# Three more places for expert weights, and an output written in eighteen contiguous pieces

## The chip, the cores and the metric

The kernel runs on one core of one Trainium2 chip. The metric is device time in microseconds (us). One run is one launch; the time before is 460.35 us, the median of three runs (460.18 to 460.82). What the host does before and after the launch, such as putting rows in order, is not part of the time.

## The reference, cut to what matters

Three layers follow one another, all in float32. `B`, `H`, `S`, `D`, `M` are 8, 8, 576, 64, 32.

```python
# 1: attention over 32 memory rows per head
a = softmax(phi)                                    # (8, 8, 576, 32)
k_m, v_m = einsum('bhsm,bhsd->bhmd', a, k), einsum('bhsm,bhsd->bhmd', a, v)
x = softmax(q @ k_m.T / 8) @ v_m                    # then to 4608 tokens x 512
# 2: maxout layer, 512 -> 768 -> 512
x = maximum(maximum(x @ w1, x @ w2), x @ w3) @ w_out
# 3: eight experts with four slots each
logits = x @ phi2                                   # 4608 x 32
slot_input = softmax(logits, axis=0).T @ x          # 32 x 512, four rows for each expert
slot_out[e] = maximum(slot_input[e] @ e_w1[e], 0) @ e_w2[e]     # 512 -> 1024 -> 512
out = softmax(logits, axis=1) @ slot_out            # 4608 x 512
```

The expert weights are 32 MB, the output is 9.4 MB. Each expert's weights meet only four rows, so the experts are little arithmetic on many bytes.

## The kernel before, in words

**The main part** (up to about 384 us of the trace) runs layers 1 and 2. Its order is written out by hand in the string `ORDER`, which names small steps one after another; each step issues a few instructions, and an engine works through its own in that order. Matmuls of `mn` (L597) fill it.

**Expert weights** are cut into 64 pieces of 512 KB, each 128 partitions by 4 KB in DRAM. The list `order` says in which sequence they are used: four `in` pieces of an expert (`e_w1`), then two `a` pieces of the expert before (the left 256 columns of `e_w2`), and at the very end sixteen `b` pieces, two for each expert (the right 256 columns). A piece goes to place `k % NSLOT` of the list `slots`. The helper `send(n)` (L279 to L287) issues the next n pieces on SP, the engine whose queue carries all transfers of this kernel; the step `send 1` in `ORDER` calls it. Places become available one after another: two of `extra` and seventeen of `arena` first, then the `late` ones, then `more2` once the pools of the main part are closed, a stretch of `hbuf` after the last sums over slots, and `wo` after the last use of the output weights of layer 2. There are 41 places, so pieces 41 to 63 reload the first 23 places when TensorE has read them. One place is a list of four buffers of 1 KB to a partition, each filled by a transfer of its own (L284). SP waits for nothing but what an instruction needs (its buffer to be free, and the transfer eight before it to have landed), and in its queue one waiting transfer holds up all behind it.

**After the main part** the last softmax over tokens is closed (L843 to L948), and the expert loop runs: `ex_in(e)` (L1016) multiplies the slots with `e_w1`, `ex_turn` transposes the result, `ex_out(e, 0)` (L1033) multiplies with the `a` pieces; one step of the softmax over slots (`c_first`, `c_second`, `c_last1`, `c_last2`) stands in each turn.

**The end** is the loop at L1110 to L1121. `so_a(x)` and `so_b(x)` (L1053, L1058 to L1060) bring half x of `slot_out` (256 columns) into two tiles `sh` and `sl`. `ex_out(r, 1)` multiplies with the `b` pieces of expert r. `st_out(r, x)` makes the rows of part r (512 tokens) and half x of the output: 12 matmuls (L1082, L1086) into four PSUM banks `x` of the pool `ps_x`, four evictions of 128x256 (two on ScalarE, L1095, two on VectorE, L1093), and a store on SP. For r below 6 each half is stored by itself (L1106: 512 KB in rows of 1 KB); for r = 6, 7, 8 both halves are collected first and stored in rows of 2 KB (L1099, L1104). The first loop runs `ex_out(r, 1)` and `st_out(r, 0)` in turn, the second `st_out(r, 1)` for all nine r. Since `ps_x` has four banks, a `st_out` takes the banks of the one before it.

Of the kernel before, what the change touches and what calls it, by code (L numbers as in the profile page):

```python
# [7 lines left out]
FP32 = mybir.dt.float32  # L8
# [14 lines left out]
for _x in (2, 3, 4, 5, 12, 6, 7, 13, 8, 9, 14, 15, 10, 11):  # L23
# [3 lines left out]
NX = 6  # L27
# [131 lines left out]
)  # L159
W = [1, 0, 0, 3, 2]  # L160
LL = 0
VP = 3
EXTRA = 2
NSLOT = EXTRA + 9 + 12 + NX + 2 + 3 + 3 + 1 + 3


@with_exitstack
def kernel(
# [87 lines left out]
    slots = [extra[:, PIECE * j:PIECE * j + PIECE] for j in range(EXTRA)]  # L256
    slots += [arena[:, o:o + PIECE] for o in slot_off]
    late_slots = [h5x[:, 0:PIECE]] + [arena[:, PIECE * j:PIECE * j + PIECE] for j in range(9)]
    late_slots += [hbuf[:, 2, 0:PIECE], arena[:, x0:x0 + PIECE]]

    order = [("in", 0)]
    for e in range(E):
# [15 lines left out]
    def send(n):  # L278
        for _ in range(n):  # L279
            if sent[0] < len(pieces):  # L280
                x = slot(sent[0])
                if isinstance(x, list):
                    for g in range(4):
                        nc.sync.dma_start(out=x[g], in_=pieces[sent[0]][:, 256 * g:256 * g + 256])  # L284
                else:
                    nc.sync.dma_start(out=x, in_=pieces[sent[0]])
                sent[0] += 1  # L287
# [519 lines left out]
    with tc.manual_schedule():  # L807
# [34 lines left out]

        main_x.close()  # L843
        more2 = ctx.enter_context(tc.tile_pool(name="more2", bufs=1, side="right"))
        more2_sb = more2.tile([128, 3 * PIECE], FP32, name="more2")
        slots.extend(more2_sb[:, PIECE * j:PIECE * j + PIECE] for j in range(3))
        send(3)
        L = B - 1
        st_logit(L, 5)
        last_logit(LL, 6)  # L850
# [62 lines left out]
        for x in range(2):  # L913
            y = mx()
            for i in range(3):
                nc.tensor.matmul(
                    y[:, 32 * i:32 * i + 32], s_run[:, 128 * (3 * x + i):128 * (3 * x + i) + 128], wsel,
                    start=True, stop=True)
            if x:
                nc.vector.tensor_copy(out=st[x], in_=y[:, 0:96])  # L920
            else:
                nc.scalar.activation(out=st[x], in_=y[:, 0:96], func=ACTF.Copy)
        nc.vector.memset(msk, 0.0)
        warm(W[2], True)
        seen = set()
# [127 lines left out]
            nc.vector.tensor_copy(out=so_sb, in_=acc[x][:, 0:256])  # L1053

        def so_b(x):
            t = mx()
            c = slice(256 * x, 256 * x + 256)
            nc.tensor.matmul(t[:, 0:256], sel, so_sb, start=True, stop=True)  # L1058
            nc.scalar.activation(out=sh[:, c], in_=t[:, 0:256], func=ACTF.Copy)
            nc.vector.tensor_tensor(out=sl[:, c], in0=t[:, 0:256], in1=sh[:, c].bitcast(FP32), op=ALU.subtract)  # L1060

        ov = out.rearrange("(g x s) c -> x s g c", x=2, s=S)
        free = [slots[64 - NSLOT + j] for j in range(NSLOT - (64 - NSLOT))]
        free = [x for x in free if not isinstance(x, list)]

        NH = 6
        tok = {}
        for r in range(9):
            tok[r] = [free.pop(0) for _ in range(1 if r < NH else 2)]

        def st_out(r, x):
            cs = slice(256 * x, 256 * x + 256)
            whole = r >= NH
            if not whole and x == 1 and free:
                tok[r] = [free.pop(0)]
            ts = [mx() for _ in range(4)]
            for k, (c, o) in enumerate(((ch, sh), (cl, sh), (ch, sl))):
                for g in range(4):
                    if r == 8 and g == 3:
                        continue  # L1080
                    rs = slice(32 * g, 32 * g + 32)
                    nc.tensor.matmul(  # L1082
                        ts[g][:, 0:256], c[rs, r], o[rs, cs], start=(k == 0), stop=(k == 2), tile_position=(32 * g, 0))
            if r == 8:
                for k, (c, o) in enumerate(((ch, sh), (cl, sh), (ch, sl))):
                    nc.tensor.matmul(ts[3][:, 0:256], c[:, 9], o[:, cs], start=(k == 0), stop=(k == 2))  # L1086
            for g in range(4):
                if whole:
                    o = tok[r][g // 2].rearrange("p (g c) -> p g c", g=2)[:, g % 2, cs]
                else:  # L1090
                    o = tok[r][0].rearrange("p (g c) -> p g c", g=4)[:, g]
                if g % 2:
                    nc.vector.tensor_copy(out=o, in_=ts[g][:, 0:256])  # L1093
                else:
                    nc.scalar.activation(out=o, in_=ts[g][:, 0:256], func=ACTF.Copy)  # L1095
                if whole and x == 1 and g % 2:
                    o = tok[r][g // 2].rearrange("p (g c) -> p g c", g=2)
                    if r < 8:
                        nc.sync.dma_start(  # L1099
                            out=out[S * r + 128 * g - 128:S * r + 128 * g + 128].rearrange("(g p) c -> p g c", p=128),  # L1100
                            in_=o)
                    else:
                        for y in range(2):
                            nc.sync.dma_start(out=ov[y, 512:576, g - 1:g + 1], in_=o[64 * y:64 * y + 64])  # L1104
            if not whole:
                nc.sync.dma_start(  # L1106
                    out=out[S * r:S * r + 512, cs].rearrange("(g p) c -> p g c", p=128),
                    in_=tok[r][0].rearrange("p (g c) -> p g c", g=4))

        so_a(0)  # L1110
        so_b(0)
        for r in range(9):
            if r < E:
                ex_out(r, 1)
            if r == E - 1:
                so_a(1)
            if r == E:
                so_b(1)
            st_out(r, 0)
        for r in [0, 1, 2, 3, 4, 5, 8, 6, 7]:  # L1120
            st_out(r, 1)  # L1121


# [57 lines left out]
```

## Time and profile before

| What | Value |
|---|---|
| median of three runs | 460.35 us |
| profiled execution, its own time | 462.82 us |
| its span, first to last instruction | 461.0 us |
| TensorE busy | 439.0 us (95%) |
| VectorE busy | 333.3 us (72%) |
| ScalarE busy | 192.4 us (42%) |
| GpSimd busy | 71.4 us (15%) |
| transfers of SP's queue, share of the 16 DMA engines | 65.2% |
| DRAM read and written | 91.38 MB, 17.30 MB |
| mean granted TensorE clock | 0.976 of 2.4 GHz |

The span is what the profiler saw between the first and the last instruction; the profiled execution took 1.8 us more than it, and 2.5 us more than the median of the unprofiled runs. The shares are means over stages with different limits, so the table says what is busy, and only the rows of a stage say what that stage waits for.

### The profile page before, as it was taken

The page shows a single profiled execution, that of the slowest core. Times are in us where ns is not written, and L with a number is a line of the kernel's source. Part 1 is how long each engine was busy: PE and PEld are TensorE (multiplying, and loading weights), DVE is VectorE, ACT ScalarE, POOL GpSimd, SP SyncE. Part 2 cuts the span into 40 slices and gives each one's busy share as a digit, 9 for nine tenths or more (in the row PEclk, how much of TensorE's full clock was granted, in tenths as well). Part 3 has the DMA queues.
Part 4 walks back from the last instruction along what each step waited for, and adds up shares of the span by engine and source line. Part 5 has one row for each costly group of instructions (what it writes and reads, how often), then busy time and mean ns, then how long its engine had stood idle before and what let it go on. Part 6 is the DMA issues. An engine that isn't in the chain of part 4 may idle for free.

```text
span 461.0 us, 12577 instructions
## 1 busy us (share of the span) xinstructions
PE 439.0 (95%) x5233; PEld 363.8 (79%) x5233; DVE 333.3 (72%) x753; ACT 192.4 (42%) x450; POOL 71.4 (15%) x92
## 2 busy tenths in 40 slices
PE   6989999999999999999999999999999999999982
PEld 5778889888887889978889698879878896654461
DVE  1596989879777986798769869899836444595441
ACT  2576766645524343334334334433433313233331
POOL 0235545620020011002100210030200000011000
PEclk9999999999999999999999999999999999999955
DMA  8987894217202395537468675388357775899988
GB/s 318 417 327 276 318 392 150 116 42 309 118 10 112 100 345 180 189 99 256 139 213 291 223 284 181 125 293 292 106 193 251 284 251 213 324 410 407 378 292 276
DMA packets 47657, 109.49 MB, mean 237 GB/s; under 512 B 3440, under 2 KB 26224, under 8 KB 45552
## 3 DMA queue, kind: packets, MB, share of 16 engines
q1 hardware_dynamic: 47600, 108.69, 65.2%
q8 instruction: 41, 0.67, 0.6%
q14 instruction: 16, 0.13, 0.1%
HBM read 91.38 MB, written 17.30 MB: 236 GB/s over the span
## 4 chain that ended last, share of the span: by engine, by line
PE 85%; DVE 5%; DMA 3%; issue 2%; ACT 2%; SPq 1%; POOL 1%; DVEq 0%; ACTq 0%; POOLq 0%
PE m L597 48%; PE x L564 7%; PE l L801 4%; PE x L439 3%; PE x L1082 3%; PE x L748 2%; DMA arena<-in_kv_dram 2%; PE x L475 2%; PE l L680 2%; PE m L1033 2%; PE m L1016 2%; PE x L639 2%; PE x L343 1%; PE l L1033 1%; SPq L663 1%
## 5 line engine op out<-in xcount | busy, mean ns | idle before, releaser
L597 PE MATMUL m<-ah,vh 128*128 128x288 f32 x576 | 171.4, 312 | 1.2 <-DVE ht L611 0.6
L597 PE MATMUL m<-ah,vl 128*128 128x288 f32 x576 | 161.8, 295 | 0.0
L597 PEld LDWEIGHTS m<-ah,vh 128*128 128x128 f32 x576 | 108.2, 188 | 20.6 <-issue 12.4
L597 PE MATMUL m<-al,vh 128*128 128x288 f32 x576 | 123.2, 295 | 0.1
L597 PEld LDWEIGHTS m<-ah,vl 128*128 128x128 f32 x576 | 108.4, 188 | 0.4
L597 PEld LDWEIGHTS m<-al,vh 128*128 128x128 f32 x576 | 92.3, 188 | 0.3 <-POOL al L532 0.3
L607 ACT ACTIVATE g<-m 128x288 f32<-128x288 f32 x96 | 38.9, 410 | 70.8 <-PE m L597 62.5
L609 DVE TENSOR_TENSOR g<-m,g 128x288 f32<-128x288 f32 x96 | 42.5, 449 | 31.0 <-PE m L597 24.4
L573 ACT ACTIVATE vh<-x 128x384 fp32r<-128x384 f32 (+1 forms) x100 | 42.0, 478 | 54.6 <-PE x L564 40.6
L611 DVE TENSOR_TENSOR ht<-m,g 128x288 f32<-128x288 f32 x96 | 42.4, 450 | 20.3 <-PE m L597 9.0
L579 DVE TENSOR_TENSOR vl<-x,vh 128x384 fp32r<-128x384 f32 (+1 forms) x100 | 48.7, 530 | 3.3 <-ACT vh L573 2.8
L564 PE MATMUL x<-arena,kvt 64*32 64x384 f32 (+1 forms) x800 | 39.5, 477 | 1.3 <-DVE vl L579 0.8
L532 POOL TENSOR_TENSOR al<-arena,ah 128x576 fp32r<-128x576 f32 x16 | 23.3, 1465 | 72.1 <-ACT ah L528 42.5
L325 POOL TENSOR_TENSOR arena<-arena 128x768 uint32<-128x768 uint32 (+1 forms) x13 | 23.5, 1808 | 34.5 <-ACT arena L313 24.2
L801 PE MATMUL l<-cst 128*128 128x128 f32 x162 | 25.0, 303 | 3.8 <-DMA cst<-in_consts_dram 3.2
L801 PEld LDWEIGHTS l<-cst 128*128 128x128 f32 x162 | 21.6, 208 | 7.1 <-DMA cst<-in_consts_dram 3.2
L616 POOL COPY arena<-ht 128x64 f32<-128x64 f32 x24 | 6.3, 279 | 124.5 <-DVE ht L611 98.9
L564 PEld LDWEIGHTS x<-arena,kvt 64*32 64x32 f32 x800 | 12.4, 105 | 13.5 <-issue 7.8
L439 PE MATMUL x<-arena 128*32 128x129 f32 x640 | 19.8, 274 | 1.1 <-DMA arena<-in_kv_dram 0.7
L643 DVE STREAM_TRANSPOSE arena<-ht 128x512 f32<-128x512 f32 x30 | 20.5, 697 | 0.2
L439 PEld LDWEIGHTS x<-arena 128*32 128x32 f32 x640 | 17.3, 110 | 3.2 <-DMA arena<-in_kv_dram 0.9
L481 DVE STREAM_TRANSPOSE arena<-x 128x288 f32<-128x288 f32 x32 | 13.3, 457 | 3.7 <-PE x L475 3.7
(246 smaller groups left out, 588.0 us busy)
## 6 DMA issues: line engine op xcount, KB each, us to landing
arena<-in_e_w_dram SPq DMA_DIRECT2D x44, 512.0 KB, 7.7
arena<-in_w_dram SPq DMA_DIRECT2D x14, 768.0 KB, 6.3
arena<-in_kv_dram SPq DMA_DIRECT2D x8, 1290.0 KB, 9.8
arena<-in_q_dram SPq DMA_DIRECT2D x16, 576.0 KB, 6.2
arena<-in_kv_dram SPq DMA_DIRECT2D x8, 1032.0 KB, 6.7
tr<-arena SPq DMA_DIRECT2D x30, 256.0 KB, 3.1
hbuf<-tr SPq DMA_DIRECT2D x30, 256.0 KB, 3.6
arena<-in_phi_t_dram SPq DMA_DIRECT2D x8, 576.0 KB, 5.9
```

The costliest lines, as they stand in the source:

```text
L325: (eng or nc.gpsimd).tensor_tensor(out=du, in0=du, in1=lo.bitcast(U32), op=ALU.add)
L439: nc.tensor.matmul(t[32 * g:32 * g + 32, 0:KVC], phin_sb[:, j, b, 32 * g:32 * g + 32], kv_sb[:, j, b, g] if j < 4 else kv4_sb[:, g], start ...
L532: nc.gpsimd.tensor_tensor(out=al[n][:, :, c], in0=aT_sb[:, :, c], in1=ah[n][:, :, c].bitcast(FP32), op=ALU.subtract)
L564: nc.tensor.matmul(t[b][32 * g:32 * g + 32, 128 * r0:128 * r1], kvt[n][r, b, 32 * g:32 * g + 32], w_sb[r, i, r0:r1, g], start=True, stop=T ...
L573: nc.scalar.activation(out=v1[n, i][0][:, b, c], in_=ph["v1", n, i][b][:, c], func=ACTF.Copy)
L579: nc.vector.tensor_tensor(out=vl[:, b, c], in0=ph["v1", n, i][b][:, c], in1=vh[:, b, c].bitcast(FP32), op=ALU.subtract)
L597: nc.tensor.matmul(t[:, 0:HALF], x, y, start=(k == 0), stop=(k == 5))
L607: nc.scalar.activation(out=g1[u, hf], in_=t[:, 0:HALF], func=ACTF.Copy)
L609: nc.vector.tensor_tensor(out=g1[u, hf], in0=t[:, 0:HALF], in1=g1[u, hf], op=ALU.max)
L611: nc.vector.tensor_tensor(out=ht[n, i][:, cs], in0=t[:, 0:HALF], in1=g1.pop((u, hf)), op=ALU.max)
L643: nc.vector.transpose(out=v, in_=ht[n, i][:, 0:512])
L801: nc.tensor.matmul(t[:, 0:128], ident, ident, start=True, stop=True)
```

## The change

1. There are 44 places. `more2` has five pieces in place of three. The place in `hbuf[:, 2]`, which was among the late ones, now comes after `more2`, and one new list of four buffers (in `s_run` and `h5x`) comes before `wo`.
2. In `ORDER` one `send 1` is gone and one stands later; `send(6)` follows the closing of the pools in place of `send(3)`.
3. The output tensor is `(2, 9, 128, 1024)`: half x, part r, partition, four groups of 256 columns. Each of the 18 pairs (r, x) is stored by one transfer of 128 rows of 4 KB, and the host puts the rows in order.
4. `ex_out(0, 1)` stands ahead of `so_b(0)`; only `st_out(0..3, 0)` stand among the `ex_out(r, 1)`; every second one of the later `st_out` uses the three banks of `ps_m` and the one of `ps_l` in place of `ps_x`.

```diff
@@ ORDER
-    "send 1; lg 7 0; mn 44 0 2; mn 44 0 0; ev 44 0 0; ev 44 1 1; ev 44 1 2; v1h 7 5; mn 44 0 1; ev 44 0 1; ev 44 "
...
+    "43 1 2; ev 43 1 1; ev 43 1 2; hrc 43; mn 45 0 1; ev 45 0 1; trm 6 5; trc 6 5; send 1; mn 47 1 0; v1h 7 4; "
...
+NH = 4
-NSLOT = EXTRA + 9 + 12 + NX + 2 + 3 + 3 + 1 + 3
+NSLOT = EXTRA + 9 + 12 + NX + 2 + 3 + 5 + 2 + 3
...
-    late_slots += [hbuf[:, 2, 0:PIECE], arena[:, x0:x0 + PIECE]]
+    late_slots += [arena[:, x0:x0 + PIECE]]
...
-        more2_sb = more2.tile([128, 3 * PIECE], FP32, name="more2")
-        slots.extend(more2_sb[:, PIECE * j:PIECE * j + PIECE] for j in range(3))
-        send(3)
+        more2_sb = more2.tile([128, 5 * PIECE], FP32, name="more2")
+        slots.extend(more2_sb[:, PIECE * j:PIECE * j + PIECE] for j in range(5))
+        slots.append(hbuf[:, 2, 0:PIECE])
+        send(6)
...
+        slots.append([s_run[:, 512:768]] + [h5x[:, PIECE + 256 * j:PIECE + 256 * j + 256] for j in range(3)])
+        send(1)
...
         def so_b(x):
-            t = mx()
+            t = bank(ps_l, "l") if x else mx()
...
+        def st_out(r, x, pool=None):
             cs = slice(256 * x, 256 * x + 256)
+            if pool:
+                ts = [bank(ps_m, "m") for _ in range(3)] + [bank(ps_l, "l")]
+            else:
+                ts = [mx() for _ in range(4)]
...
+            tok = free.pop(0)
...
-            if not whole:
-                nc.sync.dma_start(
-                    out=out[S * r:S * r + 512, cs].rearrange("(g p) c -> p g c", p=128),
-                    in_=tok[r][0].rearrange("p (g c) -> p g c", g=4))
+            nc.sync.dma_start(out=out[x, r], in_=tok)
 
         so_a(0)
+        ex_out(0, 1)
         so_b(0)
-        for r in range(9):
-            if r < E:
-                ex_out(r, 1)
-            if r == E - 1:
-                so_a(1)
-            if r == E:
-                so_b(1)
-            st_out(r, 0)
-        for r in [0, 1, 2, 3, 4, 5, 8, 6, 7]:
-            st_out(r, 1)
+        for r in range(1, E):
+            ex_out(r, 1)
+            if r <= NH:
+                st_out(r - 1, 0)
+        so_a(1)
+        st_out(NH, 0)
+        so_b(1)
+        st_out(NH + 1, 0, True)
+        rest = [(r, 1) for r in range(9)] + [(r, 0) for r in range(NH + 2, 9)]
+        for i, (r, x) in enumerate(rest):
+            st_out(r, x, i % 2)
```

How the change moves instructions shows at three places. The first is SP's queue from the last transposed tiles of the main part (`hbuf<-tr`) to the reload of `extra`; before it reads:

```order
L286 DMA arena<-in_e_w_dram 128x1024 x3
L645 DMA tr<-arena 128x512
L663 DMA hbuf<-tr 128x4x128 x5
L286 DMA hbuf<-in_e_w_dram 128x1024
L286 DMA arena<-in_e_w_dram 128x1024
L286 DMA more_5414<-in_e_w_dram 128x1024 x3
L286 DMA hbuf<-in_e_w_dram 128x1024
L286 DMA wo<-in_e_w_dram 128x1024 x3
L286 DMA extra<-in_e_w_dram 128x1024 x2
```

In the changed kernel the same stretch reads (`more_5413` is the tile `more2`):

```order
L287 DMA arena<-in_e_w_dram 128x1024
L646 DMA tr<-arena 128x512
L664 DMA hbuf<-tr 128x4x128
L287 DMA arena<-in_e_w_dram 128x1024
L664 DMA hbuf<-tr 128x4x128 x4
L287 DMA arena<-in_e_w_dram 128x1024 x2
L287 DMA more_5413<-in_e_w_dram 128x1024 x5
L287 DMA hbuf<-in_e_w_dram 128x1024 x2
L285 DMA s_run<-in_e_w_dram 128x256
L285 DMA h5x<-in_e_w_dram 128x256 x3
L287 DMA wo<-in_e_w_dram 128x1024 x3
L287 DMA extra<-in_e_w_dram 128x1024 x2
```

The piece for `hbuf`, which stood ahead of one for `arena` and three for `more2`, now stands behind both; two more pieces stand in `more2` and one in the new list, and two of the three `arena` pieces stand behind transfers of transposed tiles.

The second place is the end of SP's queue, the stores of the output; before:

```order
L1106 DMA out_dram<-arena 128x4x256 x6
L1106 DMA out_dram<-more_5414 128x4x256 x2
L1106 DMA out_dram<-hbuf 128x4x256
L1106 DMA out_dram<-wo 128x4x256 x3
L1104 DMA out_dram<-arena 64x2x512 x2
L1104 DMA out_dram<-more_5414 64x2x512 x2
L1099 DMA out_dram<-arena 128x2x512 x3
L1099 DMA out_dram<-hbuf 128x2x512
```

And with the change:

```order
L1093 DMA out_dram<-more 128x1024
L1093 DMA out_dram<-h5x 128x1024
L1093 DMA out_dram<-arena 128x1024 x10
L1093 DMA out_dram<-more_5413 128x1024 x5
L1093 DMA out_dram<-hbuf 128x1024
```

Twenty stores became eighteen of one shape, each of rows of 1024 elements (4 KB), from buffers that are all different.

The third place is TensorE's, around the second `so_b` (the matmul of `hr_96` with `cst`); before:

```order
L1033 MATMUL m<-more,hbuf 32x256
L1082 MATMUL x<-sh,ch 128x256 x4
L1082 MATMUL x<-sh,cl 128x256 x4
L1082 MATMUL x<-sl,ch 128x256 x4
L1058 MATMUL x<-hr_96,cst 128x256
L1082 MATMUL x<-sh,ch 128x256 x3
L1082 MATMUL x<-sh,cl 128x256 x3
L1082 MATMUL x<-sl,ch 128x256 x3
```

With the change:

```order
L1037 MATMUL m<-arena,hbuf 32x256 x20
L1037 MATMUL m<-more,hbuf 32x256 x4
L1081 MATMUL x<-sh,ch 128x256 x4
L1081 MATMUL x<-sh,cl 128x256 x4
L1081 MATMUL x<-sl,ch 128x256 x4
L1062 MATMUL l<-hr_96,cst 128x256
L1081 MATMUL m<-sh,ch 128x256 x3
L1081 MATMUL l<-sh,ch 128x256
L1081 MATMUL m<-sh,cl 128x256 x3
L1081 MATMUL l<-sh,cl 128x256
```

The last three `ex_out` (24 matmuls of 32x256) run without a `st_out` between them, and behind `so_b` the banks of `st_out` alternate between `x` and `m` with `l`.

## Rows read from the trace of the kernel before

**Rows 1.** Windows: start:end, length, busy time (xcount) by engine, granted clock, DMA share, GB/s.
```profile
366.00:382.00 16.00, 16.00 (x125) 15.90 (x123) 6.71 (x15) 4.17 (x10) 0.71 (x3) 1.00 0.67 215
382.00:386.00 4.00, 4.00 (x115) 3.02 (x113) 1.87 (x4) 2.19 (x5) 0.24 (x1) 1.00 0.05 8
386.00:394.00 8.00, 7.15 (x86) 4.50 (x86) 4.07 (x16) 1.77 (x7) 0.00 (x0) 1.00 0.98 385
394.00:396.00 2.00, 2.00 (x24) 1.43 (x13) 1.74 (x2) 0.38 (x1) 0.00 (x0) 1.00 0.46 133
...
400.00:404.00 4.00, 4.00 (x82) 2.43 (x76) 3.60 (x9) 1.40 (x3) 0.00 (x0) 1.00 0.87 322
404.00:426.00 22.00, 20.48 (x362) 11.00 (x354) 16.51 (x47) 7.05 (x19) 3.48 (x4) 1.00 1.03 410
426.00:438.00 12.00, 10.87 (x158) 5.86 (x150) 5.69 (x16) 4.55 (x15) 0.00 (x0) 1.00 1.06 379
438.00:440.00 2.00, 1.46 (x13) 1.15 (x13) 1.07 (x4) 0.97 (x4) 0.00 (x0) 0.68 0.48 167
440.00:452.00 12.00, 10.65 (x84) 8.24 (x84) 4.97 (x14) 4.20 (x14) 0.00 (x0) 0.50 0.95 302
452.00:454.00 2.00, 0.09 (x1) 0.00 (x0) 0.72 (x2) 0.58 (x2) 0.00 (x0) 0.50 0.93 279
454.00:458.00 4.00, 0.00 (x0) 0.00 (x0) 0.00 (x0) 0.00 (x0) 0.00 (x0) 0.50 1.03 384
458.00:461.10 3.10, 0.00 (x0) 0.00 (x0) 0.00 (x0) 0.00 (x0) 0.00 (x0) 0.50 0.41 156
```

**Rows 2.** Chain of waits, 441 to 447 us: start, length, engine, tile, line.
```profile
441.64 1.25 PE x L1082 x10
442.89 0.38 ACT wo L1095
...
443.32 1.25 PE x L1082 x10
```

**Rows 3.** Lines by shape, 440 to 448 us: evictions, xcount, busy, mean ns, idle.
```profile
L1093 DVE COPY wo<-x 128x256 f32<-128x256 f32 x6 | 2.3, 419 | 2.8 <-PE x L1082 2.8
```

**Rows 4.** Timeline of SP's issues, 384 to 462 us: start, length, line, tiles, xcount.
```profile
384.81 0.35 SPq L286 DMA_DIRECT2D hbuf<-in_e_w_dram  x1
...
390.91 0.33 SPq L286 DMA_DIRECT2D hbuf<-in_e_w_dram  x1
394.07 1.28 SPq L286 DMA_DIRECT2D wo<-in_e_w_dram  x3
...
427.71 6.57 SPq L1106 DMA_DIRECT2D out_dram<-arena  x6
```

**Rows 5.** Timeline, VectorE, 383 to 385 us: the main part's last evictions.
```profile
383.58 0.82 DVE L611 TENSOR_TENSOR ht<-m,g 128x288 f32<-128x288 f32 x2 [3.80 <-PE l L680]
```

**Rows 6.** Timeline of TensorE and the halves' tiles, 418 to 422 us.
```profile
418.26 1.07 PE L1033 MATMUL l<-arena,hbuf 128*32 128x256 f32 x16 [0.40 <-DVE hbuf L1025]
...
420.73 0.38 ACT L1059 ACTIVATE sh<-x 128x256 fp32r<-128x256 f32 x1 [0.76 <-PE x L1058]
421.14 0.42 DVE L1060 TENSOR_TENSOR sl<-x,sh 128x256 fp32r<-128x256 f32 x1 [1.21 <-ACT sh L1059]
```

**Rows 7.** Chain of waits, 416 to 438 us.
```profile
419.62 0.32 DVE hr L1053
...
419.99 0.70 PE x L1058 x2
420.69 1.00 PE m L1033 x16
421.69 0.56 PE x L1082 x12
...
431.58 1.93 PE m L1033 x15
```

**Rows 8.** Transfers, 427 to 462 us, in 40 slices: GB/s of each.
```profile
GB/s 397 391 366 379 359 380 384 384 373 377 372 376 293 118 218 349 282 330 276 339 294 335 298 320 334 304 213 248 323 220 307 358 396 407 396 386 302 26 0 0
```

More of the change, by code (lines that the diff above doesn't have):

```diff
@@ L1060, in so_b @@
             nc.vector.tensor_tensor(out=sl[:, c], in0=t[:, 0:256], in1=sh[:, c].bitcast(FP32), op=ALU.subtract)
-        ov = out.rearrange("(g x s) c -> x s g c", x=2, s=S)
         free = [slots[64 - NSLOT + j] for j in range(NSLOT - (64 - NSLOT))]
         free = [x for x in free if not isinstance(x, list)]
-        NH = 6
-        tok = {}
-        for r in range(9):
-            tok[r] = [free.pop(0) for _ in range(1 if r < NH else 2)]
-        def st_out(r, x):
+        def st_out(r, x, pool=None):
             cs = slice(256 * x, 256 * x + 256)
[L1073 to L1076, printed above, removed]
+            if pool:
+                ts = [bank(ps_m, "m") for _ in range(3)] + [bank(ps_l, "l")]
+            else:
+                ts = [mx() for _ in range(4)]
             for k, (c, o) in enumerate(((ch, sh), (cl, sh), (ch, sl))):
@@ L1086, in st_out @@
                     nc.tensor.matmul(ts[3][:, 0:256], c[:, 9], o[:, cs], start=(k == 0), stop=(k == 2))
+            tok = free.pop(0)
             for g in range(4):
[L1088 to L1091, printed above, removed]
+                o = tok[:, 256 * g:256 * g + 256]
                 if g % 2:
@@ L1095, in st_out @@
                     nc.scalar.activation(out=o, in_=ts[g][:, 0:256], func=ACTF.Copy)
-                if whole and x == 1 and g % 2:
-                    o = tok[r][g // 2].rearrange("p (g c) -> p g c", g=2)
-                    if r < 8:
-                        nc.sync.dma_start(
[L1100 to L1104, printed above, removed]
-            if not whole:
-                nc.sync.dma_start(
-                    out=out[S * r:S * r + 512, cs].rearrange("(g p) c -> p g c", p=128),
-                    in_=tok[r][0].rearrange("p (g c) -> p g c", g=4))
+            nc.sync.dma_start(out=out[x, r], in_=tok)
         so_a(0)
+        ex_out(0, 1)
         so_b(0)
-        for r in range(9):
-            if r < E:
-                ex_out(r, 1)
-            if r == E - 1:
-                so_a(1)
-            if r == E:
-                so_b(1)
-            st_out(r, 0)
-        for r in [0, 1, 2, 3, 4, 5, 8, 6, 7]:
-            st_out(r, 1)
+        for r in range(1, E):
[9 more added lines that the diff above has]
+            st_out(r, x, i % 2)
 def kernel(**inputs):
@@ L1175 @@
         args.append(nc.dram_tensor(f"in_{name}_dram", a.shape, _mybir.dt.from_np(a.dtype), kind="ExternalInput").ap())
-    args.append(nc.dram_tensor("out_0_dram", (B * S, DM), _mybir.dt.float32, kind="ExternalOutput").ap())
+    args.append(nc.dram_tensor("out_0_dram", (2, 9, 128, 1024), _mybir.dt.float32, kind="ExternalOutput").ap())
     with _tile.TileContext(nc) as tc:
@@ L1179 @@
     r = _run(nc, [arrays], core_ids=[0])
-    return r.results[0]["out_0_dram"]
+    o = _np.asarray(r.results[0]["out_0_dram"]).reshape(2, 9, 128, 4, 256)
+    res = _np.empty((B, S, 2, 256), f32)
+    res[:, 0:512] = o[:, 0:8].transpose(1, 3, 2, 0, 4).reshape(B, 512, 2, 256)
+    res[:, 512:] = o[:, 8].reshape(2, 2, 64, 4, 256).transpose(3, 1, 2, 0, 4).reshape(B, 64, 2, 256)
+    return res.reshape(B * S, DM)
```

16 rows, old and new, of the table ORDER are left out of this document.

## The prediction

> **What bounds the kernel now.** I read the windows first, stage by stage. Up to 382 us TensorE is busy in every microsecond and the transfers are not (16.00 of 16.00 us at a DMA share of 0.67), so there TensorE sets the time. From 386 us the picture turns: the share is 0.98 to 1.07 in most windows, up to 404 to 426 us, where TensorE rests for 1.5 of 22 us and the transfers run at 410 GB/s [rows 1]. What is left to move from 386 us on is countable: 32 pieces of weights (41 places, of which 32 are filled by then) and an output worth 18 pieces, 50 x 524,288 bytes. At 410 GB/s a piece takes 1.28 us and all take 63.9 us; the last bytes move at 459.5 us [rows 8], after 73.5 us. So the last part is a stream of transfers with 9.6 us lost in it, and the windows say where nearly all of it went, as length x (1 - rate/410) [rows 1]:
>
> - 394 to 396 us at 133 GB/s: 1.35 us, a hole. SP issues one piece at 390.91 us and the next at 394.07 us [rows 4], since each place comes free only then.
> - 386 to 394 us: 0.5 us. 400 to 404 us at 322 GB/s: 0.86 us; no row tells me why.
> - 426 to 438 us at 379 GB/s: 0.9 us. Here the stores in rows of 1 KB begin (issued from 427.71 us [rows 4]), with the engines as busy as they get (1.06).
> - 438 to 440 us at 167 GB/s: 1.2 us, a hole behind `so_b(1)`.
> - 440 to 452 us at 302 GB/s: 3.2 us. This is not the transfers' limit, although their share reads 0.95. The chain of waits shows `st_out` starting every 1.68 us: 1.25 us of matmuls at the half clock, then 0.38 us of eviction on ScalarE before the next may have the banks [rows 2]. 512 KB each 1.68 us is 312 GB/s, just the rate seen.
> - 452 to 459.5 us, stores in rows of 2 KB: 0.64 us and, at 384 GB/s, 0.25 us; then some 0.3 us in the last ragged stretch.
>
> Behind the last bytes lie 1.5 us to the end of the span.
>
> **The change, part by part.**
>
> *Three more places.* 33 pieces are now in by 382 us in place of 32; there is room for the extra one, at a share of 0.67 before 382 us and 0.05 after [rows 1]. The pieces moved behind `hbuf<-tr` let those transfers go sooner, and TensorE waits for neither, so the main part costs nothing more. The first piece in `more2` waits for the main part's pools, whose last user is VectorE's eviction, done at 383.58 + 0.82 = 384.40 us [rows 5]. From SP's issue at 384.81 us to moving bytes at about 386.0 us it takes 1.2 us [rows 1, 4], so the stream starts at 385.6 us, 0.4 us sooner. Seven pieces (five `more2`, two `hbuf`) cover 9.0 us, to about 395 us; `wo` follows at the latest 1.2 us behind 394.07 us plus its issues, and the new list, free after the same matmuls, stands between. Of the hole I leave 0.2 us. The list is one piece in rows of 1 KB: 1.38 us at 379 GB/s, plus 0.1 us. The wait that is added on SP is that of the list for `s_run`: `wo`, `extra` and all reloads stand behind it, but they were waiting for the same stretch of TensorE.
>
> *The stores.* 18 in rows of 4 KB. No row shows a store of that shape. The bounds: 302 GB/s below (the slowest long window of stores) and 410 GB/s above (loads with rows of 4 KB). Between stand 379 GB/s for rows of 1 KB and 384 GB/s for 2 KB, whose best slices reach 396 and 407 [rows 8]. I take 410, 1.28 us each, because the shape is that of the loads and the rate per row grows with its size: 379/1.06 = 358 GB/s per full share with 1 KB, 384/1.03 = 373 with 2 KB, 410/1.03 = 398 with 4 KB [rows 1].
>
> The Trainium skill (page "DMA: Bandwidth & Descriptors", section "Specifications") puts the least size for full line rate at 512 B, so rows of 1 KB would have nothing to gain from being longer. This case's rows speak against that, 358 to 398, but for loads against stores; by the rule the sum would come out 1.4 us later (second rival).
>
> *TensorE's order.* From `ex_out(7, 0)` at 418.26 us [rows 6], with 1.00 us for an `ex_out`, 0.56 us for a `st_out` and 0.70 us for `so_b` [rows 7]: `ex_out(7, 0)` to 419.26; `ex_out(0, 1)` to 420.26, where it covers the wait for VectorE's copy (ready at 419.94 us [rows 7]); `so_b(0)` to 420.96; seven `ex_out` and four `st_out` to 430.20. The tiles `sh` and `sl` (0.38 and 0.42 us [rows 6]) lie beside the next `ex_out`. The wait for late weights, 0.93 us of the last `ex_out` before (1.93 against 1.00 us [rows 7]), goes, since the last load lands by 427.0 us (below). Stores 0 to 3 are thus ready by about 428 us.
>
> Then `st_out(4, 0)` to 430.76, evicted by 431.6 (two evictions on VectorE, 0.42 us each [rows 3]), bytes from 432.8. `so_b(1)` to 431.46; `sh` and `sl` to 432.3; `st_out(5, 0)` needs the bank that `sl` is read from, so it ends at 432.9, is evicted by 433.7 and moves from 434.9 us.
>
> *The banks.* With two sets of banks the 0.38 us between `st_out` go: a store every 1.25 us at the half clock, or every 0.84 us at the full one (two evictions on VectorE). Both are shorter than 1.28 us: transfers bound the rest. No store waits for a buffer, all 18 being different.
>
> **The sum.** The stream: 31 loads and stores 0 to 3 are 35 x 1.28 = 44.8 us from 385.6 us, plus 0.5, 0.2, 0.1 and 0.9 us (the unexplained dip, kept): 432.1 us; the loads alone are through at 427.0 us. A hole of 0.7 us to store 4, which moves from 432.8 to 434.1 us; a second of 0.8 us to store 5. From 434.9 us 13 stores of 1.28 us: 451.5 us. With the ragged 0.3 us and 1.5 us to the end the span is **453.3 us**, 7.7 us under 461.0 us. Counted the other way, by what goes: 1.28 (one piece), 0.4 (start), 1.15 (first hole), 0.9, 3.2, 0.64 and 0.25 (stores), less 0.1 (list) and 0.3 (holes of 1.5 us in place of 1.2): 7.4 us, near enough. The profiled execution itself took 462.82 us, 2.5 us over the median of the runs; I put the difference on the median: 460.35 - 7.7 = **452.6 us**, with 451.0 to 454.3 us for this case by 410 GB/s give or take 3% and the holes give or take 1 us.
>
> Front and end are tied only at 432 to 435 us: a stream that came sooner would just find larger holes there, so the front cannot give more than 0.7 us beyond this, and could lose as much for nothing.
>
> **The rivals.**
>
> - *The rows' size does nothing* (the rule above): stores at 379 GB/s, 1.38 us each. 13 x 0.1 = 1.4 us more, 454.0 us. For it: no 4 KB store in the trace. Chance 0.10.
> - *The clock falls earlier.* Before, it is granted 1.00 in 426 to 438 us and 0.50 from 440 us on [rows 1], after TensorE had short waits; now the waits around `so_b(1)` come at 430 to 433 us. At the half clock `st_out(4, 0)`, `so_b(1)` and `st_out(5, 0)` take 0.69, 0.70 and 0.69 us more, 2.1 us: 454.7 us; the rest still keeps up at 1.25 us. Against: TensorE has no wait before 430.2 us. Chance 0.08.
> - *The places bring nothing*, as the waits only move: the 2.8 us of start, piece and hole come back, the stream reaches store 4 at 434.9 us: 2.1 us less the hole of 0.8 us, 453.9 us. Chance 0.06.
> - *Stores are at their limit already* at 302 GB/s, 1.74 us each, whatever TensorE does. Then 427.0 + 18 x 1.74 + 1.8 = 460.1 us of span, 459.4 us. For it: the share of 0.95 in that window. Against: 379 and 384 GB/s elsewhere, and the 1.68 us. Chance 0.06.
> - *Slower:* sixteen engines write rows 4 KB apart in DRAM, in place of rows 2 KB apart, and hinder one another there. It decides below (461.0 - 1.8 - 427.0)/18 = 1.79 us a store, 293 GB/s. At 270 GB/s, 1.94 us: 463.7 us of span, 463.0 us. Against it: the loads, whose rows lie the same way, run at 410. Chance 0.04.
>
> **How the numbers follow.** The forecast has the remaining 0.66, which includes small mishaps of about 1 us. The predicted time is 452.6 us. The range 450.2 to 457.0 us takes in the forecast's own, the first three rivals and 2 us beyond them for a mixture; it leaves out the last two and the far tails. A run can tell 0.2% (0.9 us) from no change. Faster: all but the slower case and half of the limit at 302 GB/s, and a little for the unforeseen, 0.91; the same 0.05; slower 0.04.
>
> **What would show it.** Right: loads end near 427 us; no window under 300 GB/s between 388 and 431 us; one or two short holes at 432 to 435 us; from there windows near 410 GB/s to about 451 us, with SP, not TensorE, last in the chain. Wrong: stores in long windows at 380 GB/s or less with the share at 1.0 (rows' size); `st_out` spaced by more than 1.3 us with idle transfers between (TensorE still the bound); a hole at 394 us again.

## The result, and the profile after

| | before | changed |
|---|---|---|
| median | 460.59 us (460.18 to 461.87, 4 runs) | 455.0 us (453.61 to 455.64, 4 runs) |
| ratio, with its 95% interval | 1 | 0.9869 (0.9846 to 0.9892) |
| profiled execution, its own time | 462.82 us | 453.61 us |
| its span | 461.0 us | 451.8 us |
| start of `ex_out(7, 0)` to the end of the span | 42.7 us | 35.6 us |
| DRAM read and written | 91.38 MB, 17.30 MB | 91.38 MB, 17.30 MB |

Faster by 5.6 us, inside the range; 452.6 us was forecast, so the gain was put too high. The profiled executions stand 9.2 us apart, more than the medians, and are no typical pair: 462.82 us lies above all 17 runs of the kernel before that stand beside e1 to e4 (459.96 to 462.31 us), and 453.61 us is the fastest of the changed kernel's four. `ex_out(7, 0)`, which began at 418.26 us [rows 6], begins at 416.16 us now: 2.1 us were won in the main part, whose TensorE work the change leaves alone. There the list of waits of the kernel before has two rows that have no counterpart in that of the changed kernel:

```profile
PEld x L439 <- DMA arena<-in_kv_dram: 0.9, 1, 0.9
PE x L439 <- DMA arena<-in_kv_dram: 0.7, 1, 0.7
```

(engine, tile and line, what was waited for, us in all, times, longest). That is 0.8 us near 260 us; the starts of equal matmuls in the two traces drift apart by 0.4 us near 8 us and by 0.7 us near 67 us as well, which makes most of the rest. It is chance and no gain of the change: the wait for `kv` is back with 0.8 or 0.9 us in the profiles of e6 and e7 (experiments, below), which share the changed kernel's main part, and e3, whose main part is that of the kernel before, starts `ex_out(7, 0)` at 417.01 us. So I measure every kernel from the start of `ex_out(7, 0)`, behind all this: 418.26 to 461.0 us before and 416.16 to 451.8 us now are 42.7 and 35.6 us, 7.1 us apart.

The windows of the changed kernel, with the columns of [rows 1]:

```profile
366.00:382.00 16.00, 16.00 (x137) 15.29 (x139) 6.34 (x16) 4.42 (x11) 0.71 (x3) 1.00 0.68 226
382.00:386.00 4.00, 3.85 (x104) 3.06 (x100) 3.04 (x11) 2.06 (x7) 0.24 (x1) 1.00 0.61 190
386.00:394.00 8.00, 7.30 (x88) 4.50 (x80) 4.13 (x9) 1.18 (x4) 0.00 (x0) 1.00 1.04 403
394.00:396.00 2.00, 2.00 (x29) 1.45 (x32) 0.41 (x2) 0.28 (x1) 0.00 (x0) 1.00 0.96 306
...
404.00:426.00 22.00, 21.41 (x378) 11.80 (x382) 15.46 (x45) 7.40 (x21) 3.50 (x4) 1.00 1.03 408
426.00:432.00 6.00, 5.38 (x89) 3.52 (x81) 3.18 (x9) 2.47 (x8) 0.00 (x0) 1.00 0.90 363
432.00:434.00 2.00, 2.00 (x37) 1.95 (x36) 2.00 (x7) 1.93 (x7) 0.00 (x0) 1.00 0.99 397
...
440.00:449.00 9.00, 0.00 (x0) 0.00 (x0) 0.02 (x1) 0.00 (x0) 0.00 (x0) 0.55 1.01 403
449.00:452.00 3.00, 0.00 (x0) 0.00 (x0) 0.00 (x0) 0.00 (x0) 0.00 (x0) 0.50 0.05 19
```

The hole of 133 GB/s at 394 us is gone (306 GB/s is left), and the stretch that ran at 302 GB/s with TensorE busy for 10.65 of 12 us [rows 1] now runs at 403 GB/s with TensorE idle: TensorE is through at 440 us and only transfers are left. In the last 3 us almost nothing moves.

The chain of waits around the second `so_b` (L1062), with start, length, engine, tile and line:

```profile
424.94 2.73 PE m L1037 x48
427.67 0.55 PE x L1081 x11
428.22 0.71 PE l L1062 x2
...
428.95 0.39 ACT sh L1063
...
429.37 0.44 DVE sl L1064
...
431.85 0.66 PE x L1081 x10
...
433.24 0.66 PE x L1081 x11
```

The last three `ex_out` run 2.73 us without a wait for weights, where one alone took 1.93 us [rows 7]. The `st_out` in banks `x` start 1.39 us apart and one in banks `m` and `l` lies between them, so a store's matmuls and evictions take 0.70 us in place of 1.68 us [rows 2]; the clock is 1.00 there.

The rates of 40 slices, 427 to 452 us, in GB/s:

```profile
GB/s 413 426 419 360 302 419 334 131 380 413 413 380 393 419 400 387 400 419 387 380 413 413 413 406 400 393 420 413 406 419 387 426 387 413 406 66 26 13 0 0
```

Two short holes at 429 and 431.5 us, then some 405 GB/s to 448.9 us. The 26 GB/s of the ragged end is one sixteenth of 410, what one of the sixteen DMA engines moves. The packets in the trace say the same: every transfer ends in sixteen packets of 4 bytes, and of those of the last store fourteen lie between 448.9 and 449.2 us, one at 449.6 and one at 450.5 us. Before, they are spread evenly from 458.7 to 459.8 us.

### The profile page after: what moved, and what is told of

The parts are those of the page before. It is cut to its first block, busy times and chain, and to the rows that moved or that the text cites. A ratio compares the mean times of both kernels' runs of the same rounds, so it can differ in the third digit from the quotient of the medians.

```text
span 451.8 us, 12570 instructions
## 1 busy us (share of the span) xinstructions
PE 430.6 (95%) x5233; PEld 359.7 (80%) x5233; DVE 333.5 (74%) x753; ACT 192.5 (43%) x450; POOL 71.4 (16%) x92
## 3 DMA queue, kind: packets, MB, share of 16 engines
HBM read 91.38 MB, written 17.30 MB: 241 GB/s over the span
## 4 chain that ended last, share of the span: by engine, by line
PE 89%; DVE 4%; issue 2%; ACT 1%; POOL 1%; DMA 1%; ACTq 0%; DVEq 0%; POOLq 0%
PE m L598 52%; PE x L565 8%; PE l L802 4%; PE x L440 4%; PE x L749 2%; PE l L681 2%; PE x L476 2%; PE m L1020 2%; PE m L1037 2%; PE x L640 2%; PE x L1081 1%; PE x L344 1%; PE l L1037 1%; PE m L1081 1%; PE x L335 1%
```

## The experiments

Each ran on the chip beside the kernel before, whose median was 461.15 us (17 runs) beside e1 to e4, 461.11 us (12) beside e5 to e8, 461.31 us (7) beside e9 to e11 and 460.67 us (11) beside e12. "Stretch" is span less start of `ex_out(7, 0)` in the timeline of TensorE.

| kernel | median, us | ratio (95% interval) | stretch, us |
|---|---|---|---|
| before | 461.15 | 1 | 42.7 |
| changed | 455.0 | 0.9869 (0.9846 to 0.9892) | 35.6 |
| e1 changed, again | 454.45 | 0.9859 (0.9843 to 0.9875) | 35.7 |
| e2 places alone | 459.73 | 0.9981 (0.9967 to 0.9995) | 41.2 |
| e3 end alone | 458.09 | 0.9947 (0.9926 to 0.9968) | 38.6 |
| e4 six `st_out` ahead | 453.45 | 0.9846 (0.9826 to 0.9866) | 34.6 |
| e5 rows of 1 KB | 457.91 | 0.9922 (0.9905 to 0.9939) | 39.2 |
| e6 four banks | 459.24 | 0.9948 (0.9925 to 0.9971) | 39.6 |
| e7 experts reversed | 454.94 | 0.9874 (0.9846 to 0.9903) | 35.9 |
| e8 reversed, six ahead | 454.29 | 0.9853 (0.9828 to 0.9878) | 35.5 |
| e9 four banks, filled | 454.55 | 0.9851 (0.9813 to 0.9888) | 36.1 |
| e10 no list | 454.07 | 0.9847 (0.9815 to 0.988) | 35.6 |
| e11 eight `st_out` ahead | 454.28 | 0.985 (0.9815 to 0.9885) | 34.4 |
| e12 no list, six ahead | 453.41 | 0.9835 (0.9805 to 0.9865) | 34.8 |

**e1: the changed kernel once more.** No edit; is the gain 5.6 or 9 us?

> The changed kernel once more, for its spread and a second profile. In the first pair of profiles the span fell by 9.2 us, of which 2.1 us lie before 382 us, in code that is the same, at three waits of the main part (about 8, 67 and 260 us; the last is TensorE waiting for a transfer of keys and values). Theory: these 2.1 us are luck of the two profiles, the change is worth what lies behind 382 us, 7 us, and the median of several runs should come to lie 5.5 to 7.5 us under the kernel before; the second profile shows one or more of the three waits again. Rival: the main part really became shorter, then every profile of the changed kernel lacks all three waits and the gain of the medians comes near 9 us.

Its ratio says 6.5 us of 461.15. `ex_out(7, 0)` starts at 417.14 us, 1.0 us later than in the first profile, and the stretch is 35.7 us again. The stretch repeats and the main part does not: of the three waits the one near 8 us is back, those near 67 and 260 us are not.

**e2: the places, with the end of the kernel before.**

```diff
-            t = bank(ps_l, "l") if x else mx()
+            t = mx()
...
-            nc.sync.dma_start(out=out[x, r], in_=tok)
+            if not whole:
+                nc.sync.dma_start(
+                    out=out[S * r:S * r + 512, cs].rearrange("(g p) c -> p g c", p=128),
+                    in_=tok[r][0].rearrange("p (g c) -> p g c", g=4))
...
-        ex_out(0, 1)
-        for r in range(1, E):
...
+        for r in range(9):
+            if r < E:
+                ex_out(r, 1)
```

> The places and their order alone: 44 places and the changed order of the pieces, with the end (stores, banks, order of TensorE) of the kernel before. Theory (stream and TensorE meet only behind the second so_b): the loads land some 2.8 us sooner and the wait of 0.93 us in the last ex_out goes, but behind it a st_out every 1.68 us bounds the end as before, so the gain is 0.9 to 1.5 us, near 459.3 us. Rival (the stream is the bound throughout): 2.8 us, near 457.7 us.

It gains 1.5 us of stretch, as the first theory said (1.4 us by the medians, 0.9 us by the ratio, whose interval reaches from 0.2 to 1.5 us). Chain of waits of e2, whose eviction is L1099 and whose `st_out` is L1086:

```profile
440.12 1.25 PE x L1086 x11
441.38 0.38 ACT more L1099
...
441.80 1.25 PE x L1086 x11
```

Still 1.68 us from one `st_out` to the next. What the earlier stream gave was given back in a wider hole: 271 GB/s in 432 to 434 us and 56 GB/s in 434 to 436 us by the windows.

**e3: the end, with the 41 places and the order of transfers of the kernel before.**

```diff
-NSLOT = EXTRA + 9 + 12 + NX + 2 + 3 + 5 + 2 + 3
+NSLOT = EXTRA + 9 + 12 + NX + 2 + 3 + 3 + 1 + 3
...
-        send(6)
+        more2_sb = more2.tile([128, 3 * PIECE], FP32, name="more2")
+        slots.extend(more2_sb[:, PIECE * j:PIECE * j + PIECE] for j in range(3))
+        send(3)
```

> The end alone: 18 stores of 4 KB rows, two sets of banks, the changed order of TensorE, with the 41 places and the order of pieces of the kernel before. Theory: the stream reaches the fourth store 2.8 us later than with the places, of which about 1 us falls into the holes there; 1.3 to 2 us slower than the changed kernel, near 456.7 us, with loads landing about 2.8 us later and almost no hole behind them. Rival (the places bring nothing, the waits only move): as fast as the changed kernel, 455.0 us. Other rival (the stream has no slack at all): 2.8 us slower, near 457.8 us.

It is 3.0 us slower than the changed kernel by the stretch (38.6 against 35.6) and 3.6 us by the medians (against e1). My theory of 1.3 to 2 us fell; that there is no slack at all, 2.8 us, was right. TensorE's timeline in e3 shows what the late stream does (the `ex_out` is L1034; in brackets the wait and its releaser):

```profile
428.18 0.64 PE L1034 MATMUL m<-more,hbuf 128*32 128x256 f32 x8 [0.67 <-DMA more<-in_e_w_dram]
429.50 0.64 PE L1034 MATMUL m<-h5x,hbuf 128*32 128x256 f32 x8 [0.69 <-DMA h5x<-in_e_w_dram]
```

The last `ex_out` wait for weights, `so_b(1)` behind them comes later, and its hole with it (303 GB/s in 434 to 436 us). So a late front moves the holes along rather than filling them. Places alone 1.5 us, end alone 4.1 us, both 7.1 us: 1.5 us come only from having both.

**e4 and e11: more stores ready before `so_b(1)`.**

```diff
-NH = 4
+NH = 6
```

(7 in e11).

> The changed kernel with st_out(0..5, 0) among the last ex_out in place of st_out(0..3, 0), so that six stores are ready while the stream still moves loads. Theory: the holes behind the second so_b (1.0 us by the windows of the changed kernel's profile, at 429 to 432 us) close, 0.7 to 1.0 us faster than the changed kernel, near 454.2 us. Rival (TensorE's chain sets the end, so_b(1) comes 1.1 us later): no gain, or up to 0.5 us slower.

> The changed kernel with st_out(0..6, 0) among the last ex_out and st_out(7, 0) ahead of the second so_b, nearly the order of TensorE of the kernel before, with the new stores and banks. Theory (with the stream as bound it only matters that stores are ready when the loads end): no holes behind 428 us, as with six ahead, 453.4 us. Rival (the changed order, with the second so_b as early as it can be, is worth something by itself): 454.5 us or slower, with a hole before the stores of the right half.

The holes nearly vanish and the stretch falls by 1.0 and 1.2 us. Windows of e4:

```profile
428.00:430.00 2.00, 2.00 (x40) 1.10 (x36) 1.21 (x4) 1.11 (x4) 0.00 (x0) 1.00 1.03 414
430.00:432.00 2.00, 1.98 (x25) 0.91 (x17) 1.41 (x4) 1.06 (x4) 0.00 (x0) 1.00 1.01 408
432.00:434.00 2.00, 1.39 (x27) 1.17 (x28) 1.25 (x4) 0.95 (x5) 0.00 (x0) 1.00 1.04 422
434.00:436.00 2.00, 2.00 (x38) 1.92 (x37) 1.98 (x6) 1.67 (x6) 0.00 (x0) 0.85 0.94 377
436.00:438.00 2.00, 2.00 (x36) 2.00 (x36) 1.52 (x5) 1.44 (x5) 0.00 (x0) 0.50 1.03 410
```

In the last row the clock is at its lower level, 0.50, and the transfers are still fed: with two sets of banks TensorE keeps up at 1.2 GHz, as the prediction had it. Two `st_out` take 1.68 us there (436.36 to 438.04 us in the chain of waits of e4), so one takes 0.84 us. In e11 the four windows from 428 to 436 us are at 416, 410, 412 and 418 GB/s. The times do not show these gains for certain: the interval of e4's ratio overlaps with that of e1, and e11's median, 454.28 us, lies within 0.2 us of e1's; in its profile `ex_out(7, 0)` starts only at 418.33 us.

**e5: the 18 stores in rows of 1 KB.**

```diff
-            nc.sync.dma_start(out=out[x, r], in_=tok)
+            v = tok.rearrange("p (g c) -> p g c", g=4)
+            nc.sync.dma_start(out=out[S * r:S * r + 512, cs].rearrange("(g p) c -> p g c", p=128), in_=v)
```

(for r = 8, two transfers of 64 partitions).

> The changed kernel, but each of its 18 stores goes to the output as it lay before, in rows of 1 KB (the last part in two transfers each); places, banks and order of TensorE as changed. Theory (the rate grows with the row): from the second so_b on the windows read 375 to 384 GB/s at a full share, 13 stores cost 0.1 us more each, 1.4 us slower than the changed kernel, near 455.9 us. Rival (the Trainium skill, page DMA: Bandwidth & Descriptors, section Specifications: rows of 512 B and more move at full line rate): the same windows near 405 GB/s and the same time, 454.5 us. Third (stores in rows of 1 KB are at their limit at 302 GB/s): 6 us slower.

Windows of e5:

```profile
438.00:440.00 2.00, 2.00 (x36) 1.67 (x35) 1.77 (x6) 1.41 (x6) 0.00 (x0) 1.00 1.05 349
440.00:442.00 2.00, 1.73 (x21) 1.28 (x17) 1.88 (x6) 1.73 (x6) 0.00 (x0) 1.00 1.03 341
...
444.00:446.00 2.00, 0.00 (x0) 0.00 (x0) 0.00 (x0) 0.00 (x0) 0.00 (x0) 0.50 1.04 341
```

The DMA engines are full (1.03 to 1.05) and move 341 to 349 GB/s, where rows of 4 KB get 403: 3.6 us more of stretch, where I expected 1.4. Some 0.6 us of this are hardly the rows': in 448 to 450 us, while a store runs that this edit splits into two transfers, the rate is 242 GB/s at a share of 0.99. The 379 GB/s from which I took that [rows 1] were a price of such stores: from 433 us on, when the last weights were in use, the kernel before moved nothing but stores in rows of 1 KB, at 374 to 385 GB/s in 433 to 437 us. So rows of 1 KB explain a loss near the one I expected, and what takes e5 from there to 341 to 349 GB/s is open; e5 stores right halves of the output in these windows, the kernel before left halves, and no run tests that. The Trainium skill (page "DMA: Bandwidth & Descriptors", section "Specifications") gives 512 B as the least size for full line rate; 1 KB is above that, and these rows do not agree with it. The edit changes the rows' length and their place in DRAM together. The packets of the traces show what the length alone does: at the median one of 1 KB takes 46 ns as a store of the kernel before (428 to 437 us) and as a load for the list in the changed kernel, 48 ns as a store in e5, one of 2 KB 84 ns (stores of the kernel before), one of 4 KB 159 ns as a load and as a store. Sixteen engines with 1024 bytes each 46 ns would move 356 GB/s, with 4096 bytes each 159 ns 412 GB/s.

**e6 and e9: four banks, empty and filled.**

```diff
-        st_out(NH + 1, 0, True)
+        st_out(NH + 1, 0)
+        fill(2)
...
-            st_out(r, x, i % 2)
+            st_out(r, x)
+            fill(2)
```

The two lines with `fill` are in e9 alone; each issues two 128x128 matmuls into a bank that nobody reads.

> The changed kernel with every st_out in the four banks of ps_x, as before. First theory (the banks give back the 3.2 us that the kernel before lost in 440 to 452 us): st_out every 1.68 us at the half clock, 312 GB/s, up to 3 us slower, near 457.5 us. Second theory: at the full clock a st_out takes 0.56 us and the wait for its banks 0.42 us, 0.98 us in all, under the 1.28 us of a transfer, so TensorE runs ahead from 431 us on; if the clock falls at 437 us it has six stores in hand, and the remaining seven at 1.68 us end at 449 us, before the transfers: 0 to 0.5 us slower, 454.5 to 455 us. The spacing of st_out in the chain of waits and windows without holes after 435 us tell.

> The kernel with every st_out in the four banks of ps_x, with two added matmuls of 128x128 into the bank of ps_l behind each st_out from the second so_b on, which nothing reads; they run while TensorE waits for its banks. Theory (four banks lose only together with the half clock: in the profile with four banks the clock fell at 435.7 us and st_out then came every 1.68 us): the clock stays at 1.00 to the end of the st_out, they come every 1.0 to 1.25 us, the windows behind 436 us read 400 to 410 GB/s, and the time is that of the changed kernel, 454.5 to 455 us. Rival (the wait for the banks is the loss at either clock): near 458 to 459 us. If the clock falls all the same, the run decides nothing.

Without the second set of banks 4.0 us are lost, more than the 3 us of the first theory; the second (0 to 0.5 us) fell. Chain of waits of e6:

```profile
433.17 0.99 PE x L1081 x11
434.16 0.38 ACT arena L1092
...
434.58 0.97 PE x L1081 x11
...
437.65 1.25 PE x L1081 x11
438.91 0.38 ACT arena L1092
...
439.33 1.25 PE x L1081 x11
```

The 1.68 us are back. But the matmuls are at half speed there: the clock is 0.85 in 434 to 436 us and 0.50 from then on. At the full clock, from 433.17 to 434.58 us, four banks cost 1.41 us a `st_out`, where the second theory had 0.98 us. e9 keeps the four banks and gives TensorE something to do during each eviction. Its timeline, with the fill on L1098:

```profile
433.70 0.71 PE L1098 MATMUL l<-cst 128*128 128x128 f32 x4
434.34 0.58 PE L1081 MATMUL x<-sh,ch 32*128 32x256 f32 x4
...
435.09 0.71 PE L1098 MATMUL l<-cst 128*128 128x128 f32 x4
```

The clock stays at 1.00 to the end of TensorE's work, a `st_out` with its fill takes 1.39 us (I expected 1.0 to 1.25 us), windows lie mostly at 358 to 399 GB/s (I expected 400 to 410), and only 0.5 us are lost against two sets. All executions agree: the mean clock is 0.974 to 0.978 in all seven of e6 and 0.999 or 1.0 in all four of e9. So four banks cost 4.0 us by two things together, the wait for the eviction (1.41 us in place of 0.70 us) and the half clock that it brings (1.68 us in place of 1.41 us); either cure takes nearly all of it.

**e7 and e8: is the dip at 394 us one of DRAM addresses?** By the bytes moved, pieces 41 to 43 ran slowly before (322 GB/s in 400 to 404 us [rows 1]), and pieces 40 to 42 run slowly after (306 GB/s in 394 to 396 us), 6 to 8 us sooner.

```diff
-        pieces += [e_w1[e, j] for j in range(4)]
+        pieces += [e_w1[E - 1 - e, j] for j in range(4)]
...
-    e_w1 = inputs["moe2_w1"].reshape(E, 4, 128, F)
+    e_w1 = inputs["moe2_w1"].reshape(E, 4, 128, F)[::-1]
```

e8 has this and `NH = 6`.

> The changed kernel with the first-layer expert weights lying in DRAM in reversed order (expert 7 first), used in the same sequence. In four profiles the transfers dip while pieces 40 to 43 move, the first-layer weights of expert 7, whatever the places they go to (400 to 404 us before, 394 to 398 us with the change). Theory (it is where these pieces lie in DRAM): the dip goes, no piece from 41 to 43 takes over 1.32 us, 0.4 to 0.8 us faster, near 453.9 us. Rival (it is the moment: transfers resuming after the main part, or what the engines do then): the dip stays at the same pieces, the same time.

> The reversed order in DRAM and six stores ahead together. Theory: the two gains add, 1.0 us for the closed holes and 0.4 to 0.8 us for the dip, since with the holes closed nothing but the stream sets the end: near 452.9 us. Rival (the dip is of the moment): 453.5 us as with six ahead alone.

The dip stays with the pieces' turn, not with their address; windows of e7:

```profile
394.00:396.00 2.00, 2.00 (x20) 1.59 (x15) 1.41 (x2) 0.38 (x1) 0.00 (x0) 1.00 0.97 331
396.00:398.00 2.00, 2.00 (x33) 1.36 (x36) 0.41 (x2) 0.28 (x1) 0.00 (x0) 1.00 0.94 301
```

e8 keeps it too (315 and 344 GB/s) and adds nothing to e4: 35.5 us against 34.6 us, slower than both its theory and its rival. The 0.9 us lie in the ragged end: over the last 5 us of the span e8 moves 125 GB/s and e4 190, which at 410 GB/s is 3.5 and 2.7 us lost.

**e10: without the list.** 43 places.

```diff
-        slots.append([s_run[:, 512:768]] + [h5x[:, PIECE + 256 * j:PIECE + 256 * j + 256] for j in range(3)])
-        send(1)
```

> The changed kernel without the new list of four buffers in s_run and h5x: 43 places. Theory (the stream sets the end): one piece more stands behind the gap in the transfers at 382 to 386 us, 1.28 us, and the piece in the list took 1.95 us in the profile where another takes 1.28 us, so 0.6 us slower than the changed kernel, near 455.1 us. Rival (the first transfers after the main part wait for places, and a place less opens the hole at 394 us again): 1.3 us or more slower, near 456 us, with a window at 394 to 396 us under 250 GB/s.

A miss: the stretch is 35.6 us as with it. The dip is still there with no piece in rows of 1 KB (348, 330 and 381 GB/s in 392 to 398 us), so the list is not its cause either. The expectation had the count wrong: the list is itself filled behind the gap at 382 to 386 us, so leaving it out puts no piece more into the stream. SP issues 31 pieces behind the gap with the list (from 382.45 us) and 31 without (from 383.05 us), and the holes behind `so_b(1)` are as large (352 and 322 GB/s in 430 to 434 us, against 365 and 301 GB/s in 428 to 432 us). Of the three new places only one takes a piece out of the stream, and the list is not that one.

**e12: no list and six ahead**, both edits of e4 and e10, run while I still held that a place less puts a piece more into the stream.

> Both edits that seemed to cost nothing or to gain: 43 places without the list, and six stores ahead. Measured from the start of the last ex_out of the left half to the end of the span, so that the luck of the main part is out of it, the changed kernel took 35.7 us in two profiles, six ahead 1.1 us less, no list the same. Theory (the list is worth nothing because what it saves in the gap it gives back in its rows of 1 KB and its four transfers; the holes are worth 1.1 us): 34.5 us from that point, near 453.3 us. Rival (with the holes closed the stream has no slack left, and the piece that then stands behind the gap costs 0.6 to 1.3 us): 35.2 to 35.9 us, near 454.2 us.

34.8 us, about e4's 34.6: the list brings nothing there either, as the equal number of pieces would have it. Windows of e12:

```profile
394.00:396.00 2.00, 2.00 (x20) 1.88 (x19) 1.15 (x4) 0.28 (x1) 0.00 (x0) 1.00 0.75 262
...
432.00:434.00 2.00, 1.66 (x32) 1.44 (x34) 1.37 (x5) 1.12 (x4) 0.00 (x0) 1.00 1.03 422
434.00:436.00 2.00, 2.00 (x40) 1.91 (x40) 2.00 (x7) 1.75 (x7) 0.00 (x0) 1.00 0.94 375
...
449.00:452.00 3.00, 0.00 (x0) 0.00 (x0) 0.00 (x0) 0.00 (x0) 0.00 (x0) 0.50 0.11 46
```

It has the lowest ratio of all, 0.9835, and beats the kernel before beyond doubt. Against the changed kernel it is 0.8 us better by the stretch, but the intervals of the ratios (0.9805 to 0.9865, and 0.9843 to 0.9875 in e1) overlap, so the times alone do not tell them apart.

## Why the prediction was right, and where it was off

Counted from `ex_out(7, 0)`, the forecast is 453.3 - 418.26 = 35.0 us to the end, and 35.6 us were measured. The last 5 us of the span, before and with the change:

```profile
456.00:461.00 5.00, 0.00 (x0) 0.00 (x0) 0.00 (x0) 0.00 (x0) 0.00 (x0) 0.50 0.67 254
446.80:451.80 5.00, 0.00 (x0) 0.00 (x0) 0.00 (x0) 0.00 (x0) 0.00 (x0) 0.50 0.46 183
```

- *The stream's start*: forecast as bound by VectorE's last eviction, 384.40 us. SP issued the first `more2` piece at 382.45 us, which is 384.55 us when the 2.1 us of the main part are put back. Right.
- *Hole and dip from 392 to 400 us*: forecast 0.2 + 0.86 us. As length x (1 - rate/410), the first 2 us of it at 368 GB/s, the next at 306, then 4 us at 388 give 0.2 + 0.5 + 0.2 = 0.9 us. Right in sum; the dip's cause is not known.
- *Rows of 4 KB at 410 GB/s*: 403 GB/s in a window of 9 us. Right, and the step on which most hung. The first rival (rows' size does nothing; in one place the prediction calls it the second) is out by these 403 GB/s and by e5; so is the fourth (stores limited at 302), and with it the slower case.
- *The banks*: 3.2 us forecast, 4.0 us by e6. The mechanism was right, but half of it was missing: I took the half clock as given, and it is a consequence of the wait. With two sets the clock was 1.00 up to 440 us; of the spacings forecast (1.25 us at half clock, 0.84 us at the full one) the second was nearer, 0.70 us measured; the first is out too, since e4 shows 0.84 us at the half clock, so the 1.25 us of [rows 2] is not what twelve matmuls cost in a row. The second rival (clock falls earlier) did not happen in the changed kernel's two profiles; in those of e4 and e10 it did. In e4 two executions with mean clocks of 0.981 and 0.982 took 452.88 and 453.83 us and two with 0.989 and 0.990 took 453.06 and 455.07 us, so no cost shows.
- *The holes around `so_b(1)`*: forecast 1.5 us. The slices of 427 to 433 us (0.625 us each) that are under 390 GB/s miss, against 410, (50 + 108 + 76 + 279 + 30)/410 x 0.625 = 0.8 us. Forecast 0.7 us too long, since at the full clock and with shorter `st_out` the second store came sooner.
- *The end of the stream*: the term that was sized wrong. "With the ragged 0.3 us and 1.5 us to the end" were 1.8 us taken from a kernel whose engines finished closer together. By the two windows above, as length x (1 - rate/410), it is 1.9 us before and 2.8 us with the change (e1 179 GB/s, 2.8 us), 1.0 us over the forecast. Less the 0.7 us above and with 0.3 us for 13 stores at 403 in place of 410 GB/s it makes the 0.6 us.
- *"The places bring nothing"*: they bring 1.5 us alone (e2) and 3.0 us with the new end (e3 against changed), where the terms said 1.28 + 0.4 + 1.15 - 0.1 = 2.7 us. Right; the remark that front and end are tied at the holes holds for e2, where the front's gain was half lost.
- *"I put the difference on the median"*: 7.7 us of span were subtracted whole from 460.35 us. The ratio of e1 on that base gives 453.9 us, so 6.5 us were won, 1.2 us less than forecast. 0.6 us of that is the stretch. The other 0.6 us lie between single profiles, whose main parts differ by up to 2.3 us (416.16 to 418.50 us among the runs), and medians; which part of it is before's profile and which the changed kernel's, no run shows.

## What to carry to other kernels

When a stage is a stream of transfers, write its losses as length x (1 - rate/full rate) window by window, and ask of each loss whether the piece before or the piece behind can use what it frees: here 1.5 of 7.1 us came only when front and end were both mended. An engine's wait may set its own clock, so price it with the clock that it will have. And compare profiles from a common point behind the parts that the edit leaves alone.

## What the runs showed of the hardware that was not expected

- A stream of 20 us does not end evenly. In the changed kernel the last packets of one store lie 1.5 us apart (448.9 to 450.5 us, at 66, 26 and 13 GB/s); e12 shows the same form (46 GB/s over the last 3 us). In the kernel before they lie 1.1 us apart, and e2, which keeps its end, moves 255 GB/s over its last 5 us, e3 with the new end 182 (254 and 183 in the kernels before and changed). Why one engine is late is open. The trace has one candidate that no run tested: other transfers, of instructions, take time from these engines, behind the last hole one of 16 KB for 0.9 us (437.8 us) and two of 8 KB for 0.3 and 0.4 us.
- Stores of 512 KB: 403 GB/s with rows of 4 KB, 341 to 349 GB/s (e5) or 374 to 385 GB/s (kernel before, 433 to 437 us) with rows of 1 KB, the share of the engines over 1.0 in all. The share says that engines are occupied, not how well: a packet of 1 KB takes 46 to 48 ns, one of 4 KB 159 ns.
- The granted clock fell in e6 after `st_out` with short waits between them (TensorE busy 1.63 and 1.34 of 2 us before and in the fall) and stayed at 1.00 in e9, where matmuls that nobody needs filled them. In e10 it fell to 0.52 in 432 to 434 us and was back at 1.00 in 436 to 438 us, in a stretch in which TensorE was busy for 2.00 of every 2 us.
- In the changed kernel some 0.9 us are lost from the eighth piece of the stream on (392 to 400 us), whatever these pieces' address (e7) and with or without a piece in rows of 1 KB among them (e10). Open.
